# Loading x by head with four neighbouring tokens per partition, and dealing the order of two stretches anew

## The chip, the cores and the metric

The kernel runs on one core of one Trainium2 chip. The metric is device time in microseconds (us) of one execution; less is better. The profile is one profiled execution; its times are in us from the start of the span unless ns is written. Engines: PE is the matrix engine, PEld its weight load, DVE the vector engine, ACT the scalar engine, POOL the GpSimd engine, SP the engine that here only issues DMAs. A `q` behind an engine's name (SPq, ACTq) means its sequencer, which issues DMAs.

## The reference

```python
# x: (B, H, S, D) = (8, 8, 512, 64)   state: (8, 8, 32, 64), all float32
scores = x @ state.T / sqrt(D);  a  = softmax(scores);   xread = a  @ state
scores2 = state @ x.T / sqrt(D); a2 = softmax(scores2);  sread = a2 @ x
# (B, H, 512+32, 64) -> (B*544, 512)
x = concat([xread, sread], axis=2).transpose(0, 2, 1, 3).reshape(B * 544, 512)
xn = x / sqrt(mean(x * x) + 1e-6) * rms_g
out = (silu(xn @ w_gate) * (xn @ w_val)) @ w_out        # d_ff = 1536
```

## The kernel before

The work goes in three stretches. The **first stretch** (0 to 139 us) handles batch 0 and turns the weights, which arrive as 64-bit numbers, into float32; it also does the attention of batch 1. Then there are seven **periods**, one for each batch from 1 to 7: the feed-forward part of batch b, and beside it the attention of batch b + 1. Last come the rows of the states of all batches together (738.6 us to the end).

Each stretch consists of independent step lists ("streams"), Python generators that each issue one or a few instructions per step. Three strings written out by hand, ORDER, PERIOD and STATES, say letter by letter which stream takes its next step. As every engine works through its instructions in the order in which they were issued, these strings fix the order on every engine's queue, the DMA queues of SP and ACT included. All seven periods use the same string PERIOD; a letter whose stream a period does not have is passed over. The streams of a period:

- `h`: the first feed-forward product, in six pairs of column blocks, each as seven products of half size (line 696; 4 matmul instructions of 256 columns each). For a pair these go to three PSUM banks x, z, y. Bank x is read by ACT after its first and second product and goes on growing.
- `t`: the copies on ACT out of these banks (lines 742, 745, 747: tile `g` twice, tile `c22`) and the silu (749). `u`: the sums and the gating on DVE (758, 771, 777, 783).
- `p`: the second product, seven products o0 to o6 of seven small ones each (line 998, 6 matmul instructions of 128 columns each). `c`: its copies on ACT (1008) into `kept`. `k`: sums on DVE, quarter_sums (1046 to 1052), half_sums (1057) and add (1038). After an add, `combine` does four sums on POOL (1024 to 1029), and then two `o` steps store the result (`store_tokens`, line 1110). The results are called p1, p5, u2 and c21, and are stored in this order.
- `v`, `w`: the products of a batch's states with w_gate and w_val (549), `x`: their copies on ACT (561) and four sums on POOL (576 to 579).
- `f`: fetches of 1 MB of these weights from DRAM (170), `g`: fetches of 576 KB of summed quarters of w_out (944), `l`: loads of a state and of x, two batches ahead. `q` and `G`, in the first period alone, make these quarters on POOL (952) and fetch the first ones.
- `a`, `s`: the attention of the next batch. From batch 2 on, x is transposed in 32x32 blocks on DVE (`xB`, 311), goes through DRAM (`x_d`, 314 and 319) and meets the states on PE (329). The last steps are the normalization (279, 435) and, with the exponentials `e` as weights, the product with x (491).

In the first stretch the letters are `a`, `s` (attention of batch 0), `A`, `S` (batch 1), `e` and `d` (the conversion of weights on ACT and DVE, lines 217 to 255), `v`, `h`, `t`, `u`, `p`, `c` (the feed-forward part of batch 0: 592, 798), `w` and `k`, and `z`: matmuls of a constant (`keep_awake`, line 1134) that only keep PE busy.

Buffers that matter here: tile `g` and the results p1, u2 and c21 share one tag with two buffers (`two`, tag "g"). A buffer that held a result is free again when both stores of it have landed. The first copy of a period (742) thus writes to a buffer that had held u2 of the period before. `w2`, the quarters, has three buffers. x of a batch has one buffer (`one`), which is free after line 491.

The x load before: four DMAs per batch, one for each group c of 128 tokens. Token 128c + p lies on partition p, as [c][head][64], in pieces of 64 numbers.

```python
x_sb[b] = (one if b else x_0).tile([P, NC, H * D], F32, name="x_b")
for c in range(NC):
    (queues or (nc.sync,))[c % max(1, len(queues))].dma_start(
        out=x_sb[b][:, c].rearrange("p (h d) -> p h d", h=H),
        in_=x[b, :, P * c:P * c + P, :].rearrange("h p d -> p h d"))
```

Of the kernel before, what the change touches and what calls it, by code (L numbers as in the profile page):

```python
# [19 lines left out]
W_BUFS = 3  # L20

ORDER = (
    "aaaaaadaaaaadeeaaeaaeadaaaeeaaaeaaadaadeaaeadddzzzzzzzzzzzzzzzzzzzzzzzzaaadaddee"
    "daaaeazzzzzzzzzzzvvzaddeadvazzzAeeadeaedzzzhtdddAehAuAhdAeAeeAAtdpdddedpddvvvhue"
    "hddeeAehddteeppdudhdededApdvpddsdtshusevevhAeedehtApdAdeAAeupeedhdAdtApddhAvAsev"
    "uvsdApdhAetdsdhphAepeAsedAtesddeesuddpAddshdudApevdvpsAvAsheeedAdthheudAedtpeAdd"
    "dAApeddAApehuvvvApedhSShtAhAdduSdhASStSpASSAASukkkSpAkwSSsswwSwpwckcSkkpkkkpckck"
    "wwww"
)

PERIOD = (
    "vxqqhthtfhthhaxhhqqquuttuxahhhththhhuuuauutthqhaaaaGthutuvqqxxvxxqxhuhhqxutuhhtu"
    "haukkthtvxqxxhhhhhuaaauutttkhhukqqqquuuathhhhhafaauutttsqauhhhhuthqqGuuusuqqqGgp"
    "upauhqqfqstuuupgppukpppppaakplpfckkkkpqakaaqqgaakkqgkcppppppppppkakkkkoakkppapsc"
    "cpkpcpggacakpsopakaappakpsakppksaaakkksppppppgkakakppakaakaookkakssppsosppcofasa"
    "wwxxxssspcwxxxloof"
)

STATES = (
# [6 lines left out]
def kernel(  # L46
# [68 lines left out]
            nc.sync.dma_start(out=rows[b][Ns * j:Ns * j + Ns], in_=src)  # L115

    def load_x(b, *queues):
        x_sb[b] = (one if b else x_0).tile([P, NC, H * D], F32, name="x_b")
        for c in range(NC):
            (queues or (nc.sync,))[c % max(1, len(queues))].dma_start(  # L120
                out=x_sb[b][:, c].rearrange("p (h d) -> p h d", h=H),
                in_=x[b, :, P * c:P * c + P, :].rearrange("h p d -> p h d"))
# [162 lines left out]
    def scores(b, packed, soft):  # L285

        xb = x_sb[b]
        stT = one.tile([P, 4, Ns], F32, name="stT")
        tp = aps.tile([P, 4, Ns], F32, name="at")
        TE.transpose(out=tp.rearrange("p j n -> p (j n)"),  # L290
                     in_=packed.rearrange("p e d -> p (e d)"), identity=ident)
        yield
        VE.tensor_copy(stT, tp)
        yield "step"

        if b < 2:
            xT = one.tile([P, 4, NC, P], F32, name="xT", tag="xT")
            for c in range(NC):
                tp = aps.tile([P, 4, P], F32, name="at")
                for j in range(4):  # L300
                    TE.transpose(out=tp[:, j, :], in_=xb[:, c, P * j:P * j + P], identity=ident)
                yield
                SE.copy(xT[:, :, c, :], tp)
                yield "step"
            xT = xT.rearrange("p j c t -> p j (c t)")
        else:


            xB = one.tile([P, 4, 4, NC, Ns], F32, name="xB", tag="xT")
            for c in range(NC):  # L310
                VE.transpose(out=xB[:, :, :, c, :].rearrange("p q j t -> p j q t"),
                             in_=xb[:, c].rearrange("p (j q t) -> p j q t", j=4, t=Ns))
                yield
            nc.scalar.dma_start(out=x_d[b % 2].rearrange("q g f r -> (g f) q r"),
                                in_=xB.rearrange("p q j c t -> p q (j c t)"))
            yield
            xT = one.tile([P, 4, 4, P], F32, name="xG", tag="xT")
            for q in range(4):
                nc.scalar.dma_start(
                    out=xT[Ns * q:Ns * q + Ns].rearrange("f g j r -> f g (j r)"),  # L320
                    in_=x_d[b % 2][q].rearrange("g f r -> f g r"))
                yield
            xT = xT.rearrange("p g j r -> p j g r")


        sp = [aps.tile([P, S], F32, name="at") for e in range(2)]
        for j in range(4):
            for e in range(2):
                TE.matmul(out=sp[e][Ns * j:Ns * j + Ns, :], lhsT=stT[D * e:D * e + D, j, :],
                          rhs=xT[D * e:D * e + D, j],  # L330
                          start=True, stop=True)
        yield


        sS = read[b] = (one if b else x_0).tile([P, 2, NC, P], F32, name="sS")
        eS = one.tile([P, 2, S // Ns, Ns], F32, name="eS", tag="eS")
        for e in range(2):
            VE.transpose(out=eS[:, e].rearrange("p k n -> p (k n)"), in_=sp[e])
            yield
            SE.copy(sS[:, e].rearrange("p c t -> p (c t)"), sp[e])  # L340
            yield "step" if e else None

        soft.update(st=stT, e=eS)
# [95 lines left out]
    def states_read(b):  # L439

        xb, sS = x_sb.pop(b), read.pop(b)
        e2 = one.tile([P, 4, 2, NC, Ns], F32, name="e2")
        exps = e2.rearrange("p g e c t -> p (g e c t)").rearrange("p (e c s) -> p e c s", e=2, s=P)
        s2 = two.tile([P, 2], F32, name="s2")
        m2 = two.tile([P, 2], F32, name="m2")
        z2 = two.tile([P, 2], F32, name="z2")
        for e in range(2):
            VE.reduce_max(out=m2[:, e:e + 1], in_=sS[:, e].rearrange("p c t -> p (c t)"),
                          axis=AXX)
            yield  # L450
        VE.tensor_scalar(s2, m2, -SCALE, None, op0=ALU.mult)
        yield
        for e in range(2):
            to = exps[:, e] if b < 2 else e2[:, :, e].rearrange("p g c t -> p g (c t)")
            SE.activation(out=to, in_=sS[:, e], func=ACTF.Exp, scale=SCALE,
                          bias=s2[:, e:e + 1], accum_out=z2[:, e:e + 1])
            yield "step" if e else None

        e2T = e2
        if b < 2:  # L460
            flat = e2T.rearrange("p j e c n -> p (j e c n)").rearrange("p (e c s) -> p e c s", e=2, s=P)
            for e in range(2):
                tp = aps.tile([P, NC, P], F32, name="at")
                for c in range(NC):
                    TE.transpose(out=tp[:, c, :], in_=exps[:, e, c, :], identity=ident)
                yield
                SE.copy(flat[:, e], tp)
                yield "step"
        else:


            eB = one.tile([P, 4, 2, NC, Ns], F32, name="eB", tag="eS")
            VE.transpose(out=eB.rearrange("p g e c n -> p (g e c n)"),
                         in_=e2.rearrange("p g e c t -> p (g e c t)"))
            yield
            nc.scalar.dma_start(out=e_d[b % 2].rearrange("j t g f -> (j t) (g f)"),
                                in_=eB.rearrange("p g e c n -> p (g e c n)"))
            yield
            for g in range(4):
                nc.scalar.dma_start(out=e2T[Ns * g:Ns * g + Ns].rearrange("t j e c n -> t j (e c n)"),  # L480
                                    in_=e_d[b % 2][:, :, g].rearrange("j t f -> t j f"))
                yield
        VE.tensor_scalar(z2, z2, 1e-9, None, op0=ALU.add)
        VE.reciprocal(z2, z2)
        yield
        rp = aps.tile([P, 2, D], F32, name="at")
        for e in range(2):
            for c in range(NC):
                for j in range(4):
                    h = 2 * j + e  # L490
                    TE.matmul(out=rp[Ns * j:Ns * j + Ns, e, :],
                              lhsT=(e2T[:, j, e, c, :] if b > 1 else
                                    flat[:, e, c, Ns * j:Ns * j + Ns]),
                              rhs=xb[:, c, D * h:D * h + D],
                              start=(c == 0), stop=(c == NC - 1))
        if b == 1:
            load_state(2)
            load_x(2)
        yield
        sr = two.tile([P, 2 * D], F32, name="sr")  # L500
        for e in range(2):
            VE.tensor_scalar(sr[:, D * e:D * e + D], rp[:, e, :], z2[:, e:e + 1], None,
                             op0=ALU.mult)
        yield
        tp = aps.tile([P, 4, Ns], F32, name="at")
        TE.transpose(out=tp.rearrange("p j n -> p (j n)"), in_=sr, identity=ident)
        yield
        VE.tensor_copy(xsT[:, :, Ns * b:Ns * b + Ns], tp)
        yield "step"
# [593 lines left out]
    def store_tokens(b):  # L1103
        def store(r, c0, n, ot):
            rows_ = out[T * b:T * b + S, c0:c0 + n]
            if b < 2:
                rows_ = rows_[P * r:P * r + P]
            else:
                rows_ = rows_.rearrange("(c g t) n -> g c t n", g=4, t=Ns)[r]
            nc.sync.dma_start(out=rows_, in_=ot)  # L1110
        return store

# [135 lines left out]
```

## Time and profile before

| | us |
|---|---|
| median of 3 runs (798.0 to 799.73) | 799.04 |
| profiled execution, its own time | 799.69 |
| its span, first to last instruction | 797.9 |
| first stretch | 0 to 139.1 |
| period of batch 1 | 139.1 to 228.5 |
| periods of batches 2 to 7 | 228.5 to 738.6 |
| of these, the middle ones (400.6 to 486.5) | 86 each |
| rows of the states | 738.6 to 797.9 |

PE is busy 95% of the span, DVE 77%, ACT 44%, POOL 37%. All six x loads of batches 2 to 7 are transfers of 256-byte pieces; 40032 of the 80035 DMA packets are under 512 bytes. In a table of waits a row reads: engine and what it was about to do, then what ended the wait, then us in total, how often, and the longest. In a timeline a row reads: start, duration, engine, line, operation, written tile and read tile, how many; in brackets the idle time before it and what ended it.

### The profile page before, as it was taken

How to read it: one execution, taken by the hardware profiler on the slowest of the kernel's cores; microseconds unless marked ns; L12 is line 12 of the kernel's file. 1: busy time of each engine (PE TensorE's matmuls, PEld its weight loads, DVE VectorE, ACT ScalarE, POOL GpSimd, SP SyncE). 2: the span in 40 equal slices, each digit the busy share in tenths (PEclk: the TensorE clock that was granted, in tenths of full speed). 3: DMA queues.
4: the chain of work that ended last, by engine and by line, in shares of the span. 5: the costliest groups of instructions: out<-in, count | busy, mean ns of one | idle time of the engine just before them, and what ended most of it. 6: DMA issues, size and time to landing. Idle time of an engine off the chain costs nothing.

```text
span 797.9 us, 14335 instructions
## 1 busy us (share of the span) xinstructions
PE 759.2 (95%) x5608; PEld 603.8 (76%) x5608; DVE 611.0 (77%) x1000; ACT 351.8 (44%) x548; POOL 292.6 (37%) x379
## 2 busy tenths in 40 slices
PE   6999999999899998999999998999899989988998
PEld 4643444778777986788777996798678868888997
DVE  4999988699947994699648993799469954788461
ACT  5798875543155423542255324542454325411220
POOL 2000004893594038312644236403840284225200
PEclk9999999999999999999999999999999999999999
DMA  9876945755896266716673557536771654052311
GB/s 285 240 261 235 313 163 137 312 173 202 263 259 209 87 226 195 247 40 233 219 241 101 195 180 256 162 105 220 202 259 43 239 186 172 1 195 70 120 53 27
DMA packets 80035, 146.17 MB, mean 183 GB/s; under 512 B 40032, under 2 KB 50784, under 8 KB 73056
## 3 DMA queue, kind: packets, MB, share of 16 engines
q1 hardware_dynamic: 66848, 125.78, 47.5%
q10 hardware_dynamic: 13120, 19.47, 8.3%
q8 instruction: 45, 0.74, 0.4%
q14 instruction: 22, 0.18, 0.1%
HBM read 116.46 MB, written 28.77 MB: 182 GB/s over the span
## 4 chain that ended last, share of the span: by engine, by line
PE 69%; DVE 20%; DMA 6%; POOL 2%; issue 2%; ACT 1%; SPq 1%; ACTq 0%; DVEq 0%; POOLq 0%
PE f L696 34%; PE f L998 11%; PE f L798 5%; PE pv L592 5%; DMA out_dram<-kept 4%; DVE hb L1057 3%; PE at L549 3%; PE f L1134 2%; PE f L861 2%; DVE kept L1038 2%; DVE h L1046 2%; DVE h L1048 2%; DVE h L1052 1%; DVE hb L771 1%; PE pv L549 1%
## 5 line engine op out<-in xcount | busy, mean ns | idle before, releaser
L758 DVE TENSOR_TENSOR g<-g,f 128x512 f32<-128x512 f32 (+1 forms) x96 | 62.0, 648 | 111.2 <-PE f L696 87.5
L696 PE MATMUL f<-aT_s,v 128*128 128x256 f32 x504 | 119.9, 385 | 0.0
L696 PEld LDWEIGHTS f<-aT_s,v 128*128 128x128 f32 x504 | 96.5, 194 | 19.4 <-issue 5.2
L696 PE MATMUL f<-aT_t,vs 128*128 128x256 f32 x336 | 88.6, 388 | 12.9 <-ACT g L742 12.9
L1024 POOL TENSOR_TENSOR kept<-kept 128x256 f32<-128x256 f32 x28 | 23.4, 835 | 200.2 <-DVE z L410 120.3
L1008 ACT COPY kept<-f 128x512 f32<-128x512 f32 (+1 forms) x56 | 29.7, 531 | 136.5 <-PE f L998 78.3
L998 PE MATMUL f<-w,h 128*128 128x128 f32 x588 | 75.5, 278 | 8.8 <-DVE h L1048 8.2
L749 ACT ACTIVATE hb<-g 128x1024 f32<-128x1024 f32 (+1 forms) x48 | 48.3, 1006 | 77.6 <-DVE g L758 77.5
L696 PEld LDWEIGHTS f<-aT_t,vs 128*128 128x128 f32 x336 | 64.2, 193 | 23.7 <-POOL kept L1026 14.7
L998 PEld LDWEIGHTS f<-w,h 128*128 128x128 f32 x588 | 69.6, 192 | 15.5 <-DVE h L1048 10.0
L272 POOL TENSOR_TENSOR ri<-ss,mhalf 128x4 f32<-128x4 f32 x8 | 11.3, 1408 | 131.5 <-DVE ss L353 117.5
L576 POOL TENSOR_TENSOR vs<-v 128x256 f32<-128x256 f32 x42 | 31.4, 746 | 75.5 <-ACT v L561 75.4
L696 PE MATMUL f<-aT_s,vs 128*128 128x256 f32 x168 | 48.4, 414 | 0.0
L696 PEld LDWEIGHTS f<-aT_s,vs 128*128 128x128 f32 x168 | 32.2, 202 | 21.0 <-issue 10.1
L747 ACT COPY g<-f 128x512 f32<-128x512 f32 (+1 forms) x48 | 26.9, 560 | 46.6 <-PE f L696 46.6
L771 DVE TENSOR_TENSOR hb<-hb,f 128x512 f32<-128x512 f32 (+1 forms) x48 | 31.2, 649 | 19.7 <-PE f L696 19.4
L696 PE MATMUL f<-aT_t,v 128*128 128x256 f32 x168 | 43.6, 382 | 1.3 <-DVE c L758 1.3
L798 PE MATMUL f<-wo,hb 128*128 128x512 f32 x96 | 44.7, 598 | 0.0
L592 PE MATMUL pv<-aT_s,v 128*128 128x512 f32 x96 | 44.2, 597 | 0.0
L998 PE MATMUL f<-wo,h 128*128 128x128 f32 x336 | 42.3, 275 | 0.0
L998 PE MATMUL f<-wo,hb 128*128 128x128 f32 x336 | 42.1, 275 | 0.0
L771 DVE TENSOR_TENSOR hb<-hb,c 128x512 f32<-128x512 f32 (+1 forms) x48 | 38.0, 791 | 3.9 <-ACT hb L749 2.9
(179 smaller groups left out, 1692.6 us busy)
## 6 DMA issues: line engine op xcount, KB each, us to landing
w_m<-w_d SPq DMA_DIRECT2D x48, 1024.0 KB
w<-t_d SPq DMA_DIRECT2D x49, 576.0 KB
x_b<-in_x_dram SPq DMA_DIRECT2D x30, 256.0 KB
out_dram<-kept SPq DMA_DIRECT2D x56, 128.0 KB
raw<-in_moe_w_val_dram SPq DMA_DIRECT2D x6, 1024.0 KB
raw<-in_moe_w_out_dram SPq DMA_DIRECT2D x6, 1024.0 KB
w_d<-w_m SPq DMA_DIRECT2D x6, 1024.0 KB
x_d<-xB ACTq DMA_DIRECT2D x6, 1024.0 KB
```

The costliest lines, as they stand in the source:

```text
L549: TE.matmul(out=pv[e][Ns * j:Ns * j + Ns, :], lhsT=stT_g[b][D * e:D * e + D, j, :], rhs=w[D * e:D * e + D, j].rearrange("p m k f -> p (m k ...
L576: GE.tensor_tensor(out=vs[:, 0], in0=a21, in1=a22, op=ALU.add)
L592: TE.matmul(out=to[0], lhsT=lhs(i, k), rhs=r, start=(i == 0), stop=(i == len(rhs) - 1))
L696: TE.matmul(out=ps[:, i, 0:half], lhsT=l[:, i, :], rhs=r, start=(start and i == 0 and k == 0), stop=(k == len(lhs) - 1), skip_group_check= ...
L747: SE.copy(gates(q)[1], q["x"][:, :, 0:half])
L749: SE.activation(out=hb[:, 2 * mp:2 * mp + 2, 0:n].rearrange("p m (c t) -> p m c t", c=2), in_=q["g"][:, :, :, 0:half], func=ACTF.Silu if s ...
L758: VE.tensor_tensor(out=to, in0=to, in1=q[ps][:, :, 0:half], op=ALU.add)
L771: VE.tensor_tensor(out=part, in0=part, in1=val, op=ALU.mult)
L798: TE.matmul(out=banks[r], lhsT=hb[:, m, P * r:P * r + P], rhs=wo[:, m, :], start=(m == 0), stop=(m == NM - 1))
L998: TE.matmul(out=to[half][:, slot, :], lhsT=lhs[:, k, :], rhs=rhs[:, k, :], start=(fresh and n in (0, 4) and k == 0), stop=(k == QM - 1), s ...
L1008: SE.copy(k[:, 4 * i:4 * i + 4 - i], banks[name][i])
L1057: VE.tensor_tensor(out=to[:, k:k + QM], in0=a[:, k:k + QM], in1=b[:, k:k + QM], op=ALU.subtract)
```

## The change

x of batches 2 to 7 is loaded in one DMA instead of four. Partition p now holds tokens 4p to 4p + 3, as [head][c][64], so that for each head four tokens stand together in 1 KB. The transposes (four per batch, as before) read two heads' halves each; line 491 reads its columns at the new place; and the stores of batches 2 to 7 put row (g, t, c) where row (c, g, t) was. Batches 0 and 1 keep their layout. ORDER and PERIOD are other strings with the same letters in the same numbers: the streams are unchanged, and their steps interleave differently.

In PERIOD, the order on SP in a middle period becomes (fetches of quarters numbered from the period's first): g1, f, g2, f, g3, g4, g5, g6, p1 twice, p5 twice, g7, u2 twice, f, x, c21 twice, f, f, state, f. Before it was: g1, f, g2, state, f, g3, g4, p1, g5, g6, p1, g7, p5 twice, u2 twice, f, four of x, c21 twice, f, f, f. The second copy of a period (742 of the second pair) now writes to a buffer that had held c21 of the period before; until now that was the third copy's.

In ORDER, 12 of the 42 `z` steps now stand at the very start; the transposes of x of batch 1 (301) and its scores (329) stand earlier; and on DVE parts of the weight conversion are mixed into the attention of batch 0. `k` steps of the first stretch stand later.

```diff
 ORDER = (
-    "aaaaaadaaaaadeeaaeaaeadaaaeeaaaeaaadaadeaaeadddzzzzzzzzzzzzzzzzzzzzzzzzaaadaddee"
-    "daaaeazzzzzzzzzzzvvzaddeadvazzzAeeadeaedzzzhtdddAehAuAhdAeAeeAAtdpdddedpddvvvhue"
-    "hddeeAehddteeppdudhdededApdvpddsdtshusevevhAeedehtApdAdeAAeupeedhdAdtApddhAvAsev"
-    "uvsdApdhAetdsdhphAepeAsedAtesddeesuddpAddshdudApevdvpsAvAsheeedAdthheudAedtpeAdd"
-    "dAApeddAApehuvvvApedhSShtAhAdduSdhASStSpASSAASukkkSpAkwSSsswwSwpwckcSkkpkkkpckck"
-    "wwww"
+    "zzzzzzzzzzzzaaaaaaaaaaaddzzzaaeeaaaaeaadzzzzzzzzzzzzzzezaaaazzzzzdadadaaeedzzzea"
+    "edzeadzazzedddaaaaaaevaAdavvAdaeAAassAAdeaaaAAeAAdddedhhtuAddhAAedAeeddhAepptuee"
+    "ddvpAvvdddeehhhdtueepeeeheppddddddtdvupedvdvhhhAddheedtuedeestApApdeeseedAAApdup"
+    "dddevvpAddvhddehAsdetsessAdhhutddAppdeeeudddspveAeeddpvAvhdeeddstedshueehAsptAAA"
+    "ddAeAAdpddhuvvSASvpSSShAtAAAheuSdeSShpddAAdAhtuSSkSwwwpwwspSSSpcccskkkkpckwwwwkk"
+    "kkkk"
 )
 PERIOD = (
-    "vxqqhthtfhthhaxhhqqquuttuxahhhththhhuuuauutthqhaaaaGthutuvqqxxvxxqxhuhhqxutuhhtu"
...
+    "vfhththahhtalhhuxxuttqqhufxtvqhhhtahahuuqquuutqhaquhaqttahhhhxthhuxquutxhuhuttuv"
+    "kkqxxxvxhaqqhhGthhqqauuuxxqqqhkaatuGhqkuuthuaattaaahuqaqhuhuthtsusushhhuutthhGug"
+    "huuqqpqtpaauufhuagpkuppkkpqsaakfgkkappcpkpakkcqkpkppapppppcqqkkkkpakppppppkppkpp"
+    "pcaaaaaksssaaqaaakpppckkpppksappkskkagggcksakaakppppaooaoposkppppgkkkpasakoawssw"
+    "xosspxfxlccoowxxxf"
 )
     def load_x(b, *queues):
+        if b > 1:
+            x_sb[b] = one.tile([P, H, NC, D], F32, name="x_b")
+            nc.sync.dma_start(out=x_sb[b].rearrange("p h c d -> p h (c d)"),
+                              in_=x[b].rearrange("h (p c) d -> p h (c d)", c=NC))
+            return
         x_sb[b] = (one if b else x_0).tile([P, NC, H * D], F32, name="x_b")
...
             xB = one.tile([P, 4, 4, NC, Ns], F32, name="xB", tag="xT")
-            for c in range(NC):
-                VE.transpose(out=xB[:, :, :, c, :].rearrange("p q j t -> p j q t"),
-                             in_=xb[:, c].rearrange("p (j q t) -> p j q t", j=4, t=Ns))
+            for q in range(4):
+                VE.transpose(out=xB[:, q], in_=xb[:, q // 2::2, :, Ns * (q % 2):Ns * (q % 2) + Ns])
                 yield
...
-                              rhs=xb[:, c, D * h:D * h + D],
+                              rhs=(xb[:, h, c, :] if b > 1 else xb[:, c, D * h:D * h + D]),
...
-                rows_ = rows_.rearrange("(c g t) n -> g c t n", g=4, t=Ns)[r]
+                rows_ = rows_.rearrange("(g t c) n -> g c t n", g=4, t=Ns)[r]
             nc.sync.dma_start(out=rows_, in_=ot)
```

More of the change, by code (lines that the diff above doesn't have):

```diff
@@ L22 @@
 ORDER = (
-    "aaaaaadaaaaadeeaaeaaeadaaaeeaaaeaaadaadeaaeadddzzzzzzzzzzzzzzzzzzzzzzzzaaadaddee"
-    "daaaeazzzzzzzzzzzvvzaddeadvazzzAeeadeaedzzzhtdddAehAuAhdAeAeeAAtdpdddedpddvvvhue"
-    "hddeeAehddteeppdudhdededApdvpddsdtshusevevhAeedehtApdAdeAAeupeedhdAdtApddhAvAsev"
-    "uvsdApdhAetdsdhphAepeAsedAtesddeesuddpAddshdudApevdvpsAvAsheeedAdthheudAedtpeAdd"
-    "dAApeddAApehuvvvApedhSShtAhAdduSdhASStSpASSAASukkkSpAkwSSsswwSwpwckcSkkpkkkpckck"
-    "wwww"
+    "zzzzzzzzzzzzaaaaaaaaaaaddzzzaaeeaaaaeaadzzzzzzzzzzzzzzezaaaazzzzzdadadaaeedzzzea"
[4 more added lines that the diff above has]
+    "kkkk"
 )
 PERIOD = (
-    "vxqqhthtfhthhaxhhqqquuttuxahhhththhhuuuauutthqhaaaaGthutuvqqxxvxxqxhuhhqxutuhhtu"
[L33 to L36, printed above, removed]
+    "vfhththahhtalhhuxxuttqqhufxtvqhhhtahahuuqquuutqhaquhaqttahhhhxthhuxquutxhuhuttuv"
[3 more added lines that the diff above has]
+    "xosspxfxlccoowxxxf"
 )
```

## The prediction

> **What bounds the kernel now.** I read the page's busy shares first: PE 95%, so only its idle time and slow time can be won. The table of waits, PE's rows picked out:
>
> ```profile
> PE f L696 <- ACT g L742: 15.6, 6, 2.7
> ...
> PE f L998 <- DVE h L1048: 8.2, 9, 1.3
> ```
>
> PE's named waits come to about 35 us: 5.8 at the start, about 5 in the period of batch 1, and 15.6 in one wait that comes six times, at the start of batches 3 to 7 and of the states (314.6, 400.6, 486.5, 572.3, 656.5, 738.6). Timeline of PE at two of them:
>
> ```profile
> 400.64 1.69 PE L696 MATMUL f<-aT_t,vs 128*128 128x256 f32 x4 [2.71 <-ACT g L742]
> 402.12 1.91 PE L696 MATMUL f<-aT_s,vs 128*128 128x256 f32 x4
> 403.82 1.33 PE L696 MATMUL f<-aT_s,v 128*128 128x256 f32 x4
> ...
> 572.27 1.10 PE L696 MATMUL f<-aT_t,vs 128*128 128x256 f32 x4 [2.44 <-ACT g L742]
> 573.21 1.03 PE L696 MATMUL f<-aT_s,vs 128*128 128x256 f32 x4
> 574.07 1.03 PE L696 MATMUL f<-aT_s,v 128*128 128x256 f32 x4
> ```
>
> At 400.64 the twelve matmuls after the wait take 4.5 us, at 572.27 they take 2.83: after five of the six waits PE also runs slow, for 1.6 us more. Who is late? The chain of waits around 486.5:
>
> ```profile
> 478.20 0.70 POOL kept L1029
> 478.90 0.02 issue
> 478.92 0.54 SPq L1110
> 479.45 0.05 issue
> 479.51 6.07 DMA out_dram<-kept
> 485.57 0.02 issue
> 485.59 0.04 ACTq L742
> ...
> 485.75 0.59 ACT g L742
> 486.34 0.14 issue
> 486.48 0.77 PE f L696
> ```
>
> The copy 742 waits for the buffer of u2, and that for u2's second store, which takes 6.07 us. It stands in a queue: the packets show 512 store packets of 1 KB (p5 twice, u2 twice) from 479.1 to 485.2, 46 ns each on four engines, 1.36 us for 128 KB. The stretches say the same: with only stores running, 0.26 of 16 engines, about four, carry 89 GB/s (columns: stretch, busy us and instructions of PE, PEld, DVE, ACT, POOL, granted clock, share of the DMA engines, GB/s).
>
> ```profile
> 480.00:481.00 1.00, 1.00 (x22) 0.36 (x28) 0.00 (x0) 0.78 (x2) 0.92 (x2) 1.00 0.26 89
> ```
>
> SP's timeline says why p5 is so late: POOL has it ready at 472.4, but its stores stand behind the last quarter fetch, which waits for its buffer until 476.11.
>
> ```profile
> 476.11 0.32 SPq L944 DMA_DIRECT2D w<-t_d  x1
> 476.53 3.51 SPq L1110 DMA_DIRECT2D out_dram<-kept  x4
> 480.14 0.45 SPq L170 DMA_DIRECT2D w_m<-w_d  x1
> 480.65 8.21 SPq L120 DMA_DIRECT2D x_b<-in_x_dram  x4
> 488.97 1.59 SPq L1110 DMA_DIRECT2D out_dram<-kept  x2
> ```
>
> **What the Trainium skill says.** "DMA: Bandwidth & Descriptors", Rules for kernel authors: an outermost dimension below 16 confines a DMA to that many engines at most. The stores of batches 2 to 7 have 4 outermost; the trace agrees (0.26 of 16). After batch 1, whose stores are 128x256, the boundary at 228.5 has no such wait. The same page, Specifications: line rate needs 512 B or more. The trace agrees: x's 256 B packets take 18.5 ns (72 ps per byte), 1 KB packets 46 ns (45). "TensorE: Matmul & The Clock Gate", Part 1: an idle window of about 3.4 us halves the clock until about 3.4 us of work. Here the half rate follows already waits of 2.7 us, five times of six, but not PE gaps of about 1 us in the period of batch 1.
>
> **The change part by part.** Times below are those of the boundary at 486.5.
>
> 1. *p5's stores go ahead of the last quarter fetch.* They then use the four engines before 479.6. The fetch (576 KB on all 16) takes 1.4 us of them, to 480.75–481.2, then u2 2 × 1.36, to 483.5–484.0, landing at 484.1 against 485.57: **−1.5** of the 2.7 per boundary. Bounds: −2.6 (all stores early; POOL's sums for this product, 483.4, come in time) and 0 (the stores queue all the same). Five boundaries, −7.5. At the sixth the streams that remain come in the same order: 0. What SP delays for this is the last quarter fetch, behind p5's issues of under 1 us each: its buffer comes free only at 476.1, which hides them.
> 2. *The half rate.* A remaining wait of 1.2 us should not bring it. Four of the five changed boundaries have it: 4 × −1.6 = **−6.4**; bounds −6.4 and 0.
> 3. *The second copy 742 gets the buffer of c21: a wait that is added.* c21's stores stand on SP behind 1 MB of w_m and all of x. From u2's last packet (483.7): w_m 8 packets × 0.31 = 2.5 us per engine, x 64 × 46–61 ns = 2.9–3.9, c21 2.7, landing 0.35: 492.2–493.2. The copy wants it when the second pair's third product comes: 485.0 + 6.2 (as before, less the half rate) + 1.9 (a `v` step between) = 493.1, less 0.75 for the copy: 492.3. Wait 0 to **+0.9**; with x as slow as today (7.6 us) the landing is 494.9 and the wait 2.6, with the half rate behind it. I take 0.9, five times: +4.5. Behind ACT's copy are its silu and DVE's gating, which have slack here (DVE busy 3.6 of 10 us in 400–410).
> 4. *x in one DMA.* SP's issue of 8.2 us shrinks to a quarter or less; its packets from 4096 × 18.5 / 16 = 4.7 us to 2.9–3.9 us. Worth nothing by itself: x is wanted a batch later. Its value is in 3.
> 5. *Transposes and 491.* 24 × 0.67 us on DVE become reads in strides. Even doubled (the nearest bound I can give; a gain isn't excluded, but DVE is off the path here), 2.7 us per batch fall into a stretch where DVE has 12.3 of 30 us free: 0. Should they move to 430–470 (DVE busy 9.7 to 10.0 of 10), each late us reaches PE. 491 reads as many numbers: 0. The stores' new rows have the same shape, 4x32x256: 0.
> 6. *State load and fetches moved on SP.* The state load goes from the third place to behind three fetches, its reader a batch away: 0. The `f` fetches have PE's slack of several us: 0, at worst 1 per period.
> 7. *ORDER.* The first real products (592) come when DVE has the attention of batch 0 ready. With conversions mixed in, DVE's chain is 13.8 us instead of 10.6; the reads come at 27.0 against 24.4 and 592 near 39.1 against 37.45: +1.65. The transposes of x of batch 1 (1.75 us of PE) are then already done: −1.75. Conversion work comes later by 0.7 us at the next val product, `v`: +0.7. Sum **+0.6**; bounds −2 (PE is warm earlier: its first 16 transposes took 0.22 us each, later ones 0.11) and +3 (every late us of DVE reaches PE, which shows no wait from 37 to 139).
> 8. *Period of batch 1.* Its waits of 5 us are for quarters made on POOL; `q` and `G` interleave otherwise. 0, bounds ±2: no view settles it.
>
> Sum: −7.5 − 6.4 + 4.5 + 0.6 = −8.8. The profiled execution took 799.69 (span 797.9 and 1.8 around it), 0.65 above the median: 790.9 on its scale, 790.3 on the median's.
>
> **The rivals.** *Both waits vanish* (0.20): u2 lands before POOL is ready and x is quick; 5 × −2.6 − 6.4 + 0.6 = −18.8, about 780. For it: without the queue a store needs 1.4 us. Against it: the fetch shares those engines. *Nothing moves* (0.10): the order on SP doesn't matter because the four engines have the same bytes to carry before u2; the layout was hidden: 799, ±1. Against it: they are partly idle from 475.7 to 477. *The wait changes its place* (0.25), slower: x's packets still take as long as today, c21's second store lands near 494.9, and the second copy waits 2.6, with 1.7 of slow PE behind it after one wait in two or after each. A boundary then loses 2.6 + 0.85 to 1.7 and saves 1.5 + 1.3 (1.6 at four of five): +0.7 to +1.5, five times +3.3 to +7.5, with ORDER's +0.6 803 to 807. It decides from a new wait of about 2 on (2 + 0.85 is what is saved): a landing at 494.3. For it: x and w_m share those same four engines ahead of c21. Against it: x is in larger packets.
>
> **How the numbers follow.** The sum case has 0.45, with a range of its own from 785 to 796 (1 and 3 each 0.9 per boundary off, 7 ±2). A measurement of this kernel can tell about 0.2%, 1.6 us, from no change. Faster: the sum case, the vanishing waits and a little of "nothing moves": 0.66. Same: most of "nothing moves": 0.08. Slower: 0.26. From 779 to 804 only the far ends of the second and the last case are left out, under 0.2.
>
> **Signs.** Right, if the row of 696 behind 742 shrinks from 2.7 to about 1.2 per boundary and a wait for 742 of the second pair, below 1 us, appears; if no twelve matmuls take 4.5 us there; if the stores of p5 are over before 479.6; if x's DMA lands in under 5 us and 24576 fewer packets are under 512 bytes. Wrong, if the second pair waits over 2 us, the granted clock still dips at the boundaries, or the first stretch ends later than 142.

## The result, and the profile after

| | before | after |
|---|---|---|
| median, us | 798.91 (6 runs) | 802.74 (6 runs) |
| ratio | | 1.0049, 95% interval 1.0034 to 1.0065 |
| profiled execution, span, us | 799.69, 797.9 | 804.48, 801.3 |
| mean granted clock of PE in it | 0.989 | 0.983 |

The kernel became half a per cent slower, and the forecast was faster. First the table of waits of PE after. The lines of the code stand 4 lower than before (5 between the load of x and the transposes): 696 is 700, 742 is 746.

```profile
PE f L700 <- ACT g L746: 13.6, 8, 2.9
PE f L1002 <- DVE h L1052: 4.3, 8, 1.2
PE at L553 <- DVE w_m L260: 4.2, 2, 2.5
PE f L700 <- POOL kept L1033: 3.2, 1, 3.2
PE f L700 <- POOL kept L1030: 2.0, 1, 2.0
```

The wait ahead of the third product is not gone. Eight waits stand in the row where there were six, and two more are put down to POOL. Those two stand at the same place: ACT's copy had waited there for its buffer as well, once for a store by the profile (658.36) and once for a sum of POOL (572.45). Ahead of 1002 the wait is half of what it was, and the largest new row, 553, lies in the first stretch. The timeline of PE at the boundary that was at 400.6:

```profile
402.75 1.10 PE L700 MATMUL f<-aT_t,vs 128*128 128x256 f32 x4 [2.10 <-ACT g L746]
...
411.21 1.10 PE L700 MATMUL f<-aT_t,vs 128*128 128x256 f32 x4 [0.85 <-ACT g L746]
```

The first wait is 2.10 instead of 2.71, and the wait that the change adds, of the second pair, is 0.85. Over the five boundaries that changed, the gaps ahead of the first pair's third product add up to 12.85 us before (2.59, 2.71, 2.51, 2.44, 2.60) and 11.89 after (1.92, 2.10, 2.63, 2.00, 3.24); those of the second pair to 4.0 (1.48, 0.85, 0.97, 0.70, none).

Where the time went is seen by setting the starts of the stretches side by side, in the two profiled executions. The first product of the period of batch 1 (696, 700) starts at 139.05 before and 143.62 after, **+4.57**. The period of batch 1 then gives back 1.40, batches 2 to 6 another 1.23, and batch 7 with the states loses 1.48: the sum is the +3.42 of the span. So the loss is made in the first stretch. The timeline of PE there:

```profile
25.77 0.81 PE L1138 MATMUL f<-ident 128*128 128x256 f32 x3
...
27.02 0.61 PE L426 MATMUL pv<-aT_s,rows 32*64 32x512 f32 x4
30.10 2.08 PE L553 MATMUL at<-w_m,stT_g 64*32 64x512 f32 x16 [2.47 <-DVE w_m L260]
32.88 0.47 PE L295 MATMUL at<-ident,rows 128*128 128x128 f32 x1 [0.70 <-ACT v L565]
33.37 1.87 PE L353 MATMUL at<-ones,sq 128*128 128x1 f32 x8
...
40.49 5.18 PE L596 MATMUL pv<-aT_s,v 128*128 128x512 f32 x8
```

Before, the sixteen matmuls of 549 took 1.09 us and the eight of 592 took 3.70; here they take 2.08 and 5.18. PE runs at half its clock for most of that time. The busy times by stretch say it outright (columns as in the prediction; the clock is the number behind the five engines). Before:

```profile
30.00:35.00 5.00, 4.62 (x35) 2.58 (x34) 4.86 (x7) 4.38 (x6) 1.51 (x1) 1.00 0.98 331
35.00:40.00 5.00, 4.50 (x16) 2.69 (x17) 4.60 (x5) 4.94 (x6) 0.42 (x1) 1.00 0.81 276
```

After:

```profile
25.00:30.00 5.00, 2.63 (x24) 1.29 (x22) 4.97 (x7) 3.06 (x6) 0.00 (x0) 1.00 0.64 210
30.00:35.00 5.00, 4.18 (x25) 2.19 (x26) 3.78 (x6) 3.00 (x4) 0.00 (x0) 0.50 0.84 276
35.00:40.00 5.00, 4.32 (x20) 3.56 (x20) 4.39 (x6) 3.27 (x5) 1.02 (x1) 0.50 0.35 143
40.00:45.00 5.00, 5.00 (x11) 2.41 (x10) 3.50 (x4) 4.09 (x5) 0.00 (x0) 0.63 0.65 208
```

PE was busy 2.63 of 5 us ahead of 30, and then had half the clock from 30.0 to 43.7, although it was busy over 80% of that time. Before, 18 `z` (36 matmuls of the constant) stood between 25.4 and 37.4:

```profile
25.39 5.02 PE L1134 MATMUL f<-ident 128*128 128x256 f32 x22
...
31.36 0.70 PE L1134 MATMUL f<-ident 128*128 128x256 f32 x2
...
33.08 1.54 PE L1134 MATMUL f<-ident 128*128 128x256 f32 x6
...
35.97 1.46 PE L1134 MATMUL f<-ident 128*128 128x256 f32 x6
```

After, none stands behind 26.6 (line 1138), since the new ORDER has moved them ahead.

### The profile page after: what moved, and what is told of

Its sections match the earlier page's. It is cut to its first block, busy times and chain, and to the rows that moved or that the text cites. A ratio compares the mean times of both kernels' runs of the same rounds, so it can differ in the third digit from the quotient of the medians.

```text
span 801.3 us, 14349 instructions
## 1 busy us (share of the span) xinstructions
PE 763.8 (95%) x5608; PEld 604.2 (75%) x5608; DVE 609.0 (76%) x1000; ACT 349.8 (44%) x548; POOL 289.8 (36%) x379
## 4 chain that ended last, share of the span: by engine, by line
PE 52%; DVE 30%; POOL 7%; issue 4%; DMA 4%; ACT 3%; SPq 0%; ACTq 0%; DVEq 0%; POOLq 0%
PE f L700 23%; PE f L1002 9%; PE pv L596 5%; PE f L802 5%; DMA out_dram<-kept 4%; DVE hb L1061 3%; DVE hb L775 3%; DVE h L1056 3%; PE at L553 2%; PE f L865 2%; DVE h L1052 2%; DVE g L762 2%; DVE h L1050 2%; DVE hs L781 2%; DVE kept L1042 2%
## 5 line engine op out<-in xcount | busy, mean ns | idle before, releaser
L700 PEld LDWEIGHTS f<-aT_t,vs 128*128 128x128 f32 x336 | 62.3, 191 | 35.7 <-issue 10.9
L580 POOL TENSOR_TENSOR vs<-v 128x256 f32<-128x256 f32 x42 | 31.7, 755 | 87.5 <-ACT v L565 87.5
L565 ACT COPY v<-pv 128x512 f32<-128x512 f32 x42 | 22.6, 592 | 81.4 <-PE pv L553 81.4
L700 PE MATMUL f<-aT_s,vs 128*128 128x256 f32 x168 | 44.7, 389 | 0.0
L751 ACT COPY g<-f 128x512 f32<-128x512 f32 (+1 forms) x48 | 26.8, 559 | 40.1 <-PE f L700 40.1
L746 ACT COPY g<-f 128x512 f32<-128x512 f32 (+1 forms) x48 | 26.7, 556 | 38.0 <-DMA out_dram<-kept 22.5
```

The source lines that it names most:

```text
L580: GE.tensor_tensor(out=vs[:, 0], in0=a21, in1=a22, op=ALU.add)
L700: TE.matmul(out=ps[:, i, 0:half], lhsT=l[:, i, :], rhs=r, start=(start and i == 0 and k == 0), stop=(k == len(lhs) - 1), skip_group_check= ...
L746: SE.copy(gates(q)[0], q["x"][:, :, 0:half])
L751: SE.copy(gates(q)[1], q["x"][:, :, 0:half])
```

## The experiments

Each kernel was timed in three rounds beside the kernel before; the medians of before were 798.72 (first four), 799.15 (next four) and 799.56 (last four).

**One part alone.** The four kernels take their strings and their layout from either kernel:

```diff
 e1: after,  with ORDER and PERIOD of before
 e2: before, with ORDER of after
 e3: after,  with ORDER of before
 e4: before, with PERIOD of after
```

e1, the layout alone.

> The new x layout, load, transposes and store rows, with the ORDER and PERIOD of before. Theory (the loss is ORDER's, the layout is cover only): 0 within 1.5 us of before; the wait of 742 stays at 2.4 to 2.7 us at six boundaries, because the stores in front of u2 are the same. Rival (the layout costs on its own: strided transposes on DVE, or x's single transfer pushing u2's or c21's stores about): over 2 us slower, to be seen as new waits of PE for xG or DVE. A gain over 2 us would say that x's quicker transfer matters in the old order too.

Measured: 802.44, ratio 1.0074 (1.0048 to 1.0099). Slower, as the rival says, but not for its reasons: the waits of 742 stay (2.04 to 3.03), no wait of PE for xG or for the transposes appears, and these take what they took (683 ns each, 682 before). The clock isn't the reason either: its mean over these runs is 0.992, against 0.989 before. What is new is a wait at the *second* pair, 0.70 at 322.87 and 1.53 at 580.52; the chain of waits there:

```profile
574.16 5.54 DMA out_dram<-kept
...
579.79 0.59 ACT g L746
580.39 0.14 issue
580.52 1.53 PE f L700 x6
```

The second pair's copy stands for c21's second store (SP issues both from 573.56 on, behind x): it has got the buffer of c21, which the third pair's had before. No edit is near these buffers, and what shifted them is not shown. Nor is this all of the loss. The two new waits are 2.2 of the 4.2 us by which the profiled span is longer; another 1.6 lie behind ACT's last copy (797.10 to 802.1, before 794.47 to 797.9), where the last stores land later, and why they do stays open.

e2, ORDER alone.

> The kernel before with the new ORDER only. Theory: first real product (592) near 40.5, end of the first stretch 4.6 us later, and at least part of it kept to the end: +3 to +4.6 us. Rival: the 1.4 us that the period of batch 1 gives back in the changed kernel belong to ORDER (quarters and fetches are ready when a late period starts), then +3.2. If PERIOD or layout caused the late first stretch: 0.

Measured: 803.79, ratio 1.0089 (1.0052 to 1.0126): +5.1 us. The first 592 starts at 38.74 and the first stretch ends 2.83 late in the profiled execution, less than expected; the clock is at half from 31.7 to 41.9. Over its runs the mean granted clock is 0.980, against 0.989 before: 0.009 of 804 us are 7 us at full rate, so the clock alone would account for ORDER's loss. The run after the next two tests it.

e3, PERIOD and layout.

> The changed kernel with the ORDER of before: PERIOD and layout alone. Theory: first 592 again at 37.45 and the first stretch ends at 139; the periods keep what they have in the changed kernel: 1.1 to 2.6 us faster than before. Rival (the periods' gain came only from starting late): no faster than before, within 1 us.

Measured: 799.71, ratio 1.0012 (0.9988 to 1.0035): no difference. The first stretch is as before (592 at 37.63), so the loss is ORDER's, and the rival holds for the rest: within 2 us or so, PERIOD and layout together are worth nothing as they stand. Its profiled execution was 793.77 with a clock of 0.995, one of the quick ones of its runs (793.8 to 804.1), and is not to be taken for the median.

e4, PERIOD alone.

> The kernel before with the new PERIOD only (x still in four DMAs of 256 B pieces). Theory: c21's stores stand behind x; with 256 B pieces the wait of the second pair's 742 is 1.5 us or more longer than in the changed kernel (0.7 to 1.5 there), so 5 boundaries x 1.5 and some slow PE: 5 to 12 us slower than the run of PERIOD with the layout. Rival (x's size is hidden here too): equal to that run within 1.5 us.

Measured: 801.51, ratio 1.0042 (1.0023 to 1.0061), 1.8 above e3: less than the theory has, and a little more than the rival. Here too the second pair's copy waits for c21, and longer than in e3: the three waits over 0.3 us add up to 4.0 (0.55, 1.67, 1.79), in e3 to 2.0 (1.19, 0.42, 0.40). The 1 KB rows seem to be worth something to this wait, not 5 us.

**Was it the `z`?**

```diff
 ORDER = (
-    "zzzzzzzzzzzzaaaaaaaaaaaddzzzaaeeaaaaeaadzzzzzzzzzzzzzzezaaaazzzzzdadadaaeedzzzea"
-    "edzeadzazzedddaaaaaaevaAdavvAdaeAAassAAdeaaaAAeAAdddedhhtuAddhAAedAeeddhAepptuee"
+    "aaaaaaaaaaaddzzzaaeeaaaaeaadzzzzzzzzzzzzzzezaaaazzzzzdadadaaeedzzzeaedzeadzazzed"
+    "ddazzzzzaaaaaevzzaAdavvAdazzzeAAassAAdeaaaAAeAAdddedzzhhtuAddhAAedAeeddhAepptuee"
...
```

> The changed kernel, with the 12 z that stand at the very start of its ORDER moved to the later gaps of PE (5 behind the reads of batch 0, 2 behind the first v, 3 behind 353, 2 ahead of the first 596). Theory: the changed kernel loses to PE's clock, which is at half from 30.0 to 43.7 us because no z stands there any more; with z there the half rate in that stretch is gone, first 596 near 38.5 and the whole about 4.5 us faster than the changed kernel, 798. Rival: DVE, which has conversions mixed into the attention of batch 0, is late anyway: first 596 stays at 40 or later, no faster than 801.

Measured: 797.99, ratio 0.9997 (0.9970 to 1.0024), 4.7 below the changed kernel. The expectation holds, and the clock is whole again (the third number from the right):

```profile
30.00:35.00 5.00, 4.64 (x32) 3.82 (x31) 4.51 (x8) 3.07 (x6) 1.02 (x1) 1.00 0.98 337
35.00:40.00 5.00, 4.13 (x20) 2.60 (x19) 4.81 (x5) 4.98 (x6) 0.00 (x0) 1.00 0.21 54
```

The first 596 starts at 37.78, against 40.49, and the first stretch ends 0.30 behind before's. The mixed conversions, which the prediction charged with 1.65, cost next to nothing once PE has its clock (first 596 0.33 later than before). The same twelve steps of idle matmuls that bring nothing at the start are worth 4.7 us some 25 us later.

**Take the waits on stores away.** No copy 742 may wait for a store when `g` has a buffer that no result uses:

```diff
-                q["g"] = two.tile([P, 2, 2, HS], F32, name="g", tag="g")
+                q["g"] = two.tile([P, 2, 2, HS], F32, name="g", tag="gg", bufs=1)
...
-        m1 = two.tile([P, 2, S // Ns], F32, name="m1")
+        m1 = two.tile([P, 2, S // Ns], F32, name="m1", bufs=1)
...
-        seven["vs"] = ctx.enter_context(tc.tile_pool(name="sums", bufs=3))
+        seven["vs"] = ctx.enter_context(tc.tile_pool(name="sums", bufs=2))
```

(`z1` as `m1`; the smaller buffers pay for the 4 KB per partition.) e6 is the kernel before with this.

> The kernel before, with tile g of the periods in a buffer of its own (tag gg, one buffer), so that no copy 742 waits for a store; paid for with sums in two buffers instead of three and m1, z1 in one. Theory (PE waits for the stores alone, and the half rate follows that wait): six waits of 2.6 and the slow stretches behind them are gone, 15 us of waiting and 5 to 8 of slow PE: 776 to 780. Rival (POOL's sums 577 or another releaser are late by nearly as much): waits of 1 us or more stay at the same place with another releaser, 786 to 795.

Measured: 779.15, ratio 0.9747 (0.9711 to 0.9783). All six waits and every stretch of half rate but the last microseconds are gone; the granted clock is 1.000 in all its runs. The rival's other releaser does not come at that place. What is left: ACT is held up twice at its own transfer of x through DRAM (the chains at 334.7 and 418.6 show 10.79 and 10.96 us of `x_d<-xB` ahead of a copy), and PE waits 1.66 and 1.11.

e7 is e3 with this edit.

> PERIOD and layout of the changed kernel with the ORDER of before, and tile g in a buffer of its own as in the last. Theory: with both waits on stores gone, PERIOD and layout keep what the period of batch 1 and the small waits of 998 gained (1.8 and 0.5 per period): 2 to 4 us faster than the kernel before with its own g. Rival (the strided layout or the later x_d round trip costs PE): no faster than it, waits ahead of the scores (333) of 0.2 to 0.5 us each.

Measured: 773.78, ratio 0.9696 (0.9661 to 0.9732), 5.4 below e6. The boundary now runs through, all eight matmuls of two products in a row:

```profile
389.45 1.13 PE L700 MATMUL f<-aT_s,v 128*128 128x256 f32 x4
390.42 2.03 PE L700 MATMUL f<-aT_t,vs 128*128 128x256 f32 x8
392.29 0.27 PE L295 MATMUL at<-ident,rows 128*128 128x128 f32 x1
```

So PERIOD and layout do bring something, which the two waits on stores had taken back. It has the lowest median of the study (e9 and e12 below can't be told from it).

**Use all DMA engines for the stores.** e8 is the kernel before, with

```diff
-            nc.sync.dma_start(out=rows_, in_=ot)
+            if b < 2:
+                nc.sync.dma_start(out=rows_, in_=ot)
+                return
+            for c in range(NC):
+                nc.sync.dma_start(out=rows_[c], in_=ot[Ns * c:Ns * c + Ns])
```

> The kernel before, with every store of batches 2 to 7 issued as four DMAs of 32 partitions (one per token group), which can spread over all 16 engines, instead of one with 4 outermost. Theory (four engines in series hold u2 up): u2 lands 2 us or more earlier, the waits of 742 fall below 1 us, the half rate behind them goes: 780 to 786. Rival (SP's issue, 0.54 us per DMA and 24 more per period, takes the engines' place): u2's eight DMAs are issued over 4.3 us, landing near 484 to 485, and what stands behind them on SP is late: 794 to 800.

Measured: 806.58, ratio 1.0098 (1.0067 to 1.0130): the rival, and worse. The chain at the same boundary:

```profile
482.52 0.42 SPq L1114
...
485.05 0.41 SPq L1114
485.46 0.06 issue
485.51 1.62 DMA out_dram<-kept
...
488.24 0.89 PE f L696 x3
```

A store lands 1.62 us after its last issue instead of queueing for 6; but SP needs until 485.5 to issue p5's and u2's sixteen, and PE waits 3.80.

**Which part gains once the stores are out of the way?** All with `g` in its own buffer: e9 with PERIOD alone, e10 with the layout alone, e11 the whole change, e12 as e11 with the `z` of e5.

> The kernel before with tile g in its own buffer, and the new PERIOD only (old layout, old ORDER). Theory: without the waits on stores, what the periods gain (0.5 us per period ahead of 998, about 1 in the period of batch 1) is PERIOD's own: 774 to 776, against 779 with the old PERIOD. Rival (the gain is the layout's, by x's or x_d's transfers): 778 to 780.

Measured: 774.44, ratio 0.9687 (0.9640 to 0.9735). As the theory says.

> Tile g in its own buffer, the new layout only (ORDER and PERIOD of before). Theory: the layout costs 3.7 us by itself only because the second pair's copy gets the buffer of c21; with g in its own buffer that is gone and the layout is worth 0: 777 to 780. Rival (the layout costs PE in another way, strided transposes or the way through x_d): 782 or more. A gain of 3 us or more would give the layout what theory gives to PERIOD.

Measured: 775.71, ratio 0.9696 (0.9654 to 0.9737). The layout no longer costs anything. It even lies 3.4 under e6, which the expectation had at 0; these are four runs each, timed in different rounds. The long waits of e6 behind `x_d` are absent in e9 and e10 alike, which is why the two gains do not add up: 4.7 and 3.4, together 5.4 (e7). Which transfer frees them wasn't taken apart.

> The changed kernel as it is, its ORDER too, with tile g in its own buffer. Theory: ORDER's loss is in the first stretch (half rate from 30 to 44 us) and independent of the waits on stores: 774 + 4.5 = 778 to 779. Rival (a late first stretch is made good in the period of batch 1): 775 or less.

Measured: 777.73, ratio 0.9726 (0.9687 to 0.9766): 4.0 above e7. The clock is at 0.50 from 30 to 40 us as in the changed kernel, and the period of batch 1 doesn't make it good.

> The last with the 12 z of the start moved to PE's later gaps. Theory: the half rate from 30 to 44 is gone and nothing else is left of ORDER: 773 to 775, as with the old ORDER. Rival (the mixed conversions make DVE late): 776 or more.

Measured: 774.87, ratio 0.9696 (0.9651 to 0.9741), 2.9 below e11 and within a run's spread of e7 and e9.

## Why the prediction was wrong

- **Step 7 (ORDER, +0.6) failed, and decides the sign.** It counted what DVE and PE have to do and when, with a gain for a PE that is warm earlier, but gave the `z` no worth where they had stood. Without them PE is idle for 2.47 us ahead of 30.10 and in pieces behind that, and runs at half its clock for 13.7 us. Measured +4.57 at the end of the stretch; e5 gets 4.7 us back by moving 12 `z`, e11 and e12 2.9 in the other setting. The conversions' +1.65 and +0.7 were not needed to explain it.
- **Step 1 (stores earlier, −7.5) failed on a term of its sum.** The four engines were to carry p1's and p5's four stores, the last fetch and u2's two in 9.6 us from 473.9 on. SP issues them in the order foreseen (the lines below; 944 and 1110 are 948 and 1114 after). A count of packets has the stores begin at 475.5 (the same point, 1.6 later) and end near 486.5: 11 us. The 1.4 us too little are the gain of 1.5. About half of them is arithmetic: 128 packets of 46 ns on four engines are 1.47 us for a store, and the prediction took 1.36, which makes 0.7 us for six. The rest is a start that is not steady: in the first 2 us the stores come at 12 to 47 in half a microsecond. The fetch's packets trickle between them up to 484.3. The waits fell by 0.2 each, 1.0 in all. The order in the queue was moved as foreseen, but the same six stores stood together, and this order did not make the queue shorter.

```profile
473.23 2.85 SPq L1114 DMA_DIRECT2D out_dram<-kept  x4
477.72 0.33 SPq L948 DMA_DIRECT2D w<-t_d  x1
480.10 1.39 SPq L1114 DMA_DIRECT2D out_dram<-kept  x2
```

- **Step 2 (half rate gone, −6.4) failed in its reason.** It took the length of a wait for what decides. Waits of 1.9 to 2.6 stayed, and yet after four of the five no half rate came; it came after 659.09 (a wait of 3.24) and after 740.60 (2.90), for twice as long each, 6.8 us. A wait of 2.63 brought none after, one of 2.51 did before. In e3, waits of 2.0 to 3.1 brought it after two of six. The last section shows what it goes by. That four of the five were spared, as foreseen, is luck: the waits had not become shorter by more than 0.7. Over all six boundaries 17.1 us at half rate became 13.7, which saves 1.7 us.
- **Step 3 (the second copy behind c21, +0.9 each) was right:** 0.8 on average. The layout alone and PERIOD alone each put that copy on c21's buffer (e1, e4).
- **Step 4 (x in one DMA) was right that it is worth nothing to PE, but not in its reason.** x's issue takes 0.42 us on SP instead of 8.2. But x is wanted much sooner than a batch later: DVE's first transposes of it start at 493.32, 11.1 us behind its issue, and have waited 0.59 us for it. A landing in under 5 us, named as a sign of being right, did not come.
- **Steps 5 and 6 were right:** the strided transposes take 702 ns instead of 682, and nothing of the moved loads shows in PE's waits.
- **Step 8 (0 ± 2):** −1.4, and it is PERIOD's (−1.2 in e3 with the old ORDER).

Of the signs of being wrong two came: the first stretch ended at 143.62, later than 142, and the clock still dipped at boundaries. By size, steps 1 and 2 are the larger miss: without ORDER the sum was −9.4, and e3 measured +1.0 (−1.0 to +2.8). ORDER turned that nothing into a loss.

The rival "the wait changes its place" named 803 to 807, near the 802.74 measured, but by luck: the new wait is 0.8, not over 2, and the loss stands in the first stretch. Where the expected gain is, e6 and e7 show: 20 us lay in the waits on stores and the slow PE behind them, and they go when the copy doesn't share a buffer with a result, not when the stores are dealt anew.

## What to carry to other kernels

Idle matmuls that keep the matrix engine awake are work like any other when an order is dealt anew: look where the clock would fall without them, not only at what waits. When a wait ends with a transfer out of a shared buffer, try a buffer of its own first: it took 2.5% here, while moving the transfers in their queue gave nothing and splitting them cost 1%. After any edit of tiles or orders, compare which store each copy waits for; a layout change alone brought a wait to a copy that it never touched.

## What the runs showed of the hardware

Most of the spread between runs of the kernel before goes with the clock. Over its 46 runs, the time lies between 790.6 and 806.3 us and falls by 0.75 us for each 0.001 of mean granted clock (correlation −0.90); 0.001 of 800 us is 0.8 us. With `g` in its own buffer and the old ORDER the clock is 0.997 to 1.000. Not all of it does: e6's four runs, all at 1.000, still lie 4.3 us apart.

The half rate comes in pieces of 3.4 us or multiples (3.4 at five places before; 6.8 twice and 13.7 once after), so the same wait of 2 to 3 us costs 0, 1.7 or 3.4 us. Within each of the fourteen traces, all changes of the clock lie on one grid with intervals of 3.41 us, which no wait shifts. What decides is how much of a wait falls into one interval. Two waits of the kernel before, 2.59 ahead of 314.60 and 2.44 ahead of 572.27, by the intervals of its grid (columns as above: PE's busy time comes first behind the comma, the clock behind the five engines):

```profile
312.27:315.69 3.42, 1.09 (x5) 1.02 (x6) 0.00 (x0) 1.07 (x2) 3.26 (x6) 1.00 0.87 242
315.69:319.10 3.41, 3.41 (x11) 2.60 (x10) 0.75 (x2) 2.36 (x3) 3.25 (x6) 0.50 0.59 132
568.28:571.69 3.41, 1.55 (x8) 1.02 (x6) 0.00 (x0) 0.53 (x2) 3.25 (x6) 1.00 1.02 337
571.69:575.10 3.41, 2.83 (x14) 2.51 (x15) 0.67 (x1) 2.60 (x5) 3.25 (x6) 1.00 0.57 146
```

The first leaves PE idle for 2.33 us of one interval, and the next is at half rate; the second is cut in two by the grid, with 1.86 us in the first interval, and nothing happens. Over all traces, from 20 us on, 31 of the 32 falls to half rate followed an interval in which PE was idle for 1.98 us or more (one, in e2, 1.84), and none of the 3044 intervals at full rate that were followed by another had over 1.96. The way back asks for more: an interval at half rate in which PE was idle for 0.62 us or more was followed by another, one with up to 0.51 us by the full rate. Three intervals with no idle time (0.01 at most) were followed by another too (33.42 to 36.83 after, and its like in e2 and e11); they hold transposes and products of one column. So from 30.0 to 43.7 us a PE that was busy for over 80% was not granted the full clock again.

The Trainium skill, "TensorE: Matmul & The Clock Gate", Part 1, has the window of about 3.4 us and calls it free-running, so that the point of a change varies from run to run; the grid of 3.41 us agrees. It names a whole idle window as what halves the clock; here about 2 us of one were enough.
